# A gated MLP on one core: the DMA transposes of x take 256 columns in place of 128

## The chip, the core and the metric

The kernel runs on one core of a Trainium2 chip. The core has five engines that run side by side: TensorE (matrix products, PE in the profile; its weight loads are the row PEld), VectorE (DVE), ScalarE (ACT), GpSimd (POOL) and SyncE (SP), which in this kernel issues every DMA. Sixteen DMA engines move the data between the chip's main memory (HBM) and the on-chip memory. The metric is the device time of one execution in microseconds (us); lower is better.

## The reference

For x of 2048 rows by 1024 columns and three weight matrices, all bf16:

```
g = x @ w_gate          # 2048 x 3584
u = x @ w_up            # 2048 x 3584
h = gelu(g) * u         # gelu in its tanh form
out = h @ w_down        # 2048 x 1024
```

## The kernel before, in words

Both stages use Strassen's scheme, in which a product of 2x2 blocks needs seven block products and a number of sums of blocks (the tiles s1 to s4 are sums of weight blocks, t1 to t4 sums of blocks of x). The sums are made by VectorE and GpSimd, copies out of TensorE's accumulators (the eight banks) mostly by ScalarE.

The 2048 rows of x are taken as two passes p of 1024, and each pass as two halves c of 512 rows. TensorE contracts over the partition dimension, so x is needed transposed: for each (p, c) eight blocks, one for each 128 of the 1024 columns, each a tile of 128 partitions by 512 rows of x. They are kept in `XT[p, c][ko]`, ko from 0 to 7 (lines 72, 73 and 87 to 94):

- (0, 0) lies in xT0. It is turned by TensorE itself at the start (`turn`, L798), from four plain loads `xn`.
- (0, 1) lies in four slots `x` of two blocks each.
- (1, 0) lies in xT1, and (1, 1) in the first eight of the fourteen rows of the tile h01, which is used for other things later.

The last three are filled by DMA transposes, 24 in all, each 512 rows by 128 columns, issued on SyncE's queue by `transposing` (L806). The order of that queue is the order of the program. At its head stand the four loads of xn, the loads of the weights for the first block of columns (L814, in three parts) and the second one (L145). Then come the eight transposes of (0, 1), the loads of the third block of weights (L143), and the sixteen transposes of pass 1. The list `turns` (L833) gives the order of these sixteen: first blocks 0 to 3 of (1, 1) and (1, 0) in turn, then blocks 4 to 7 of (1, 1), then blocks 4 to 7 of (1, 0). `turn_some(n)` issues the next n of the list: four at once (L840), the others between steps of the first two units of work, by the table `AHEAD` (L48), where (n, part) is the unit and the place within it. Between these groups the queue holds the stores of finished blocks of h to HBM (L227, in `times`), each of which waits for VectorE to have written its block.

Who reads the transposed blocks around these steps:

- `plain` (L842) multiplies blocks by the first weights, two blocks of x after each other for each of four accumulators.
- `sums_t` (L153) makes t1 to t4 of pass 0 on VectorE, a block at a time, and casts blocks 4 to 7 of (0, 1) on ScalarE (tb).
- `two_sums` (L938) makes t1 to t4 of pass 1 on GpSimd, two blocks in an instruction.
- `product` (L229) with `raw_first` and `raw_second` (L233, L238) takes four blocks in order for each of two accumulators: blocks 0 to 3 of xT1, then 4 to 7. In the second unit (n is 1 in `ahead_of_p4`, L1087) the first such products of pass 1 run: 16 on blocks 0 to 3, then eight on blocks 4 to 7, four for each accumulator.

After these first units the kernel goes on with joint units for both passes up to some 385 us, and then with the second product, out = h @ w_down.

Of the kernel before, what the change touches and what calls it, by code (L numbers as in the profile page):

```python
# [10 lines left out]
def kernel(  # L11
# [13 lines left out]
    P = nc.NUM_PARTITIONS  # L25
# [7 lines left out]
    x2 = x.flatten_outer_dims()  # L33
# [4 lines left out]
    NKB = Dm // P  # L38
    KH = NKB // 2
    NFB = Df // P  # L40
    NJ = NFB // 2
    N = 512
    NS = N // P
    NPASS = S // (2 * N)
    NU = NFB // 2
    NWARM = 7
    JOINT = 3
    AHEAD = {(0, -2): 4, (0, -1): 2, (0, 0): 2, (0, 1): 2, (1, -2): 2}  # L48
    DIVIDED7 = 5
    STAY = range(11, 14)  # L50
    KEEPS = [(u, n) for u in range(5, NU) for n in range({7: 2, 9: 2, 11: 2, 13: 3}.get(u, 1))]
# [19 lines left out]

    xT = [xpool.tile([P, NKB, N], bf16, name=f"xT{p}") for p in range(NPASS)]
    XT = {(p, 0): [xT[p][:, k] for k in range(NKB)] for p in range(NPASS)}
    h = [[None, None], [None, None]]

    wdn = w_down.rearrange("(kh j p) d -> p kh j d", kh=2, p=P)

    def slot(shape, dtype, name):
        return kpool.tile(shape, dtype, name=name, tag="k")
# [7 lines left out]
    def late_half(p):  # L87
        if p:
            tile = hpool.tile([P, NJ, N], bf16, name="h01")
            XT[p, 1] = [tile[:, k] for k in range(NKB)]  # L90
            x_late.append(tile[:, :NKB])
        else:
            tiles = [slot([P, 2, N], bf16, "x") for _ in range(KH)]
            XT[p, 1] = [tiles[k // 2][:, k % 2] for k in range(NKB)]

    def new_h(kh, c):
        h[kh][c] = hpool.tile([P, NJ, N], bf16, name=f"h{kh}{c}")
# [20 lines left out]
    def snap(ps, name):  # L118
        t = slot([P, N], f32, name)
        nc.scalar.copy(out=t, in_=ps)  # L120
        return t
# [10 lines left out]
    def load_w(u, slots=False):  # L132
        f0 = u * 2 * P
        if slots:
            w = [[slot([P, KH, 2 * P], bf16, "w") for _ in range(2)] for _ in range(2)]
        else:
            tile = wpool.tile([P, 2, NKB, 2 * P], bf16, name="w")
            w = parts(tile)
        for i, src in enumerate((w_gate, w_up)):
            src = src[:, f0 : f0 + 2 * P].rearrange("(ko ki) f -> ki ko f", ki=P)  # L140
            if slots:
                for half in range(2):
                    nc.sync.dma_start(out=w[i][half], in_=src[:, half * KH : (half + 1) * KH])  # L143
            else:
                nc.sync.dma_start(out=tile[:, i], in_=src)  # L145
        return w
# [6 lines left out]
    def sums_t(p, eng, place):  # L153
        K = range(KH)
        lo, hi = [[XT[p, c][k0 : k0 + KH] for c in range(2)] for k0 in (0, KH)]

# [72 lines left out]
    def product(ps, lhs, rhs, start):  # L229
        for k in range(KH):  # L230
            matmul(ps, lhs[:, k, :], rhs[k], start and k == 0, k == KH - 1)

    def raw_first(e, p, w):  # L233
        for i in range(2):
            product(e[i], w[i][0][:, :, :P], XT[p, 0][:KH], True)
        return [snap(e[i], "p1") for i in range(2)]

    def raw_second(c, p, w):  # L238
        for i in range(2):
            product(c[i], w[i][1][:, :, :P], XT[p, 0][KH:], True)  # L240

# [110 lines left out]
    def joint_ops(u, E, F):  # L352
# [28 lines left out]
        def raw(name, p, i):  # L381
            ops["P1" + name] = lambda: product(E[p][i], w[i][0][:, :, :P], XT[p, 0][:KH], True)

# [419 lines left out]
            ks = slice(ks.start, ks.stop)  # L803
            (on_act if i == 1 else on_dve)(out=xT[0][:, ks, i * P : (i + 1) * P], in_=tp[:, ks])

    def transposing(p, c, ko):  # L806
        r0 = (2 * p + c) * N
        nc.sync.dma_start_transpose(  # L808
            out=XT[p, c][ko], in_=x2[r0 : r0 + N, ko * P : (ko + 1) * P]
        )  # L810

    def load_wf(queue, k0, k1):
# [12 lines left out]
    for k0, k1 in ((0, 2), (2, 5), (5, NKB)):  # L825
        load_wf(nc.sync, k0, k1)
    w = load_w(1)
    late_half(0)
    for ko in range(NKB):
        transposing(0, 1, ko)  # L830
    ahead = load_w(2, True)
    late_half(1)
    turns = [(c, ko) for ko in range(KH) for c in (1, 0)] + [(c, ko) for c in (1, 0) for ko in range(KH, NKB)]  # L833

    def turn_some(n):
        for c, ko in turns[:n]:
            transposing(1, c, ko)
        del turns[:n]

    turn_some(4)  # L840

    def plain(ps, c, kos, parts=1):  # L842
        n = N // parts
# [221 lines left out]
    with tc.manual_schedule(engines={ENG.Activation}):  # L1065
        for n, (u, p) in enumerate(items):
# [4 lines left out]
            def aside(part):  # L1071
# [4 lines left out]
                for v in loads.get((n, part), ()):  # L1076
                    ws[v] = load_w(v, True)
                turn_some(AHEAD.get((n, part), 0))
                if (n, part) == (1, -2):
# [125 lines left out]
```

## Time and profile before

| what | value |
|---|---|
| runs shown (three) | 530.77, 529.16, 531.03 us, median 530.77 |
| profiled execution | 528.45 us |
| its span, first to last instruction | 526.7 us |
| granted TensorE clock | 1.000 |
| TensorE busy | 520.9 us (99%) |
| GpSimd, VectorE, ScalarE busy | 337.5, 390.6, 293.9 us |
| DMA transposes: x, h01, xT1 | 8 each, first issue 8.4 us, last 47.4 us |
| one of them on SyncE's queue, median | 1.25 to 1.26 us |
| from issue to landing, shortest, median, longest | 2.5, 2.9, 5.9 us |

The profile is of one execution. In the rows a line like L124 is the line of the kernel's source; a line such as L124, L103 or L106 is a helper that records most of TensorE's, VectorE's or GpSimd's operations, so groups are told apart by their tiles (`bank<-xT,w` reads xT and w and writes an accumulator). "SPq" is SyncE's queue: the time of an issue is how long the instruction held the queue, and the landing of the data comes after it. An arrow in brackets, as in `[1.03 <-DMA xT<-in_x_dram]`, gives the idle time ahead of the row and what ended it. The chain of work that ended last is followed back from the last instruction, at each step to what released it. In the tables of windows the columns are the window, its length, then the busy time and number of instructions of TensorE, its weight loads, VectorE, ScalarE and GpSimd, the granted clock, the mean busy share of the DMA engines and GB/s.

### The profile page before, as it was taken

The page shows a single profiled execution, that of the slowest core. Times are in us where ns is not written, and L with a number is a line of the kernel's source. Part 1 is how long each engine was busy: PE and PEld are TensorE (multiplying, and loading weights), DVE is VectorE, ACT ScalarE, POOL GpSimd, SP SyncE. Part 2 cuts the span into 40 slices and gives each one's busy share as a digit, 9 for nine tenths or more (in the row PEclk, how much of TensorE's full clock was granted, in tenths as well). Part 3 has the DMA queues.
Part 4 walks back from the last instruction along what each step waited for, and adds up shares of the span by engine and source line. Part 5 has one row for each costly group of instructions (what it writes and reads, how often), then busy time and mean ns, then how long its engine had stood idle before and what let it go on. Part 6 is the DMA issues. An engine that isn't in the chain of part 4 may idle for free.

```text
span 526.7 us, 7917 instructions
## 1 busy us (share of the span) xinstructions
PE 520.9 (99%) x2389; PEld 367.9 (70%) x2389; DVE 390.6 (74%) x598; ACT 293.9 (56%) x542; POOL 337.5 (64%) x339
## 2 busy tenths in 40 slices
PE   8999999999999999999999999999999999999997
PEld 4575777767677676767676676754688885488887
DVE  2984553587888889897988899896879226966934
ACT  2545655767687686878787786851135601142430
POOL 1169899999999999999999999940000000000694
PEclk9999999999999999999999999999999999999999
DMA  9755233042625266363727354999986999983732
GB/s 245 161 133 131 73 110 110 21 120 76 205 70 191 83 218 209 120 217 113 257 96 229 136 184 145 338 371 415 386 273 200 392 402 371 394 307 101 237 132 71
DMA packets 103114, 105.91 MB, mean 201 GB/s; under 512 B 19744, under 2 KB 81184, under 8 KB 103072
## 3 DMA queue, kind: packets, MB, share of 16 engines
q1 hardware_dynamic: 103072, 105.41, 61.1%
q8 instruction: 19, 0.31, 0.3%
q14 instruction: 23, 0.19, 0.1%
HBM read 72.61 MB, written 29.62 MB: 194 GB/s over the span
## 4 chain that ended last, share of the span: by engine, by line
PE 91%; SPq 3%; DVE 2%; DMA 2%; issue 1%; ACT 0%; DVEq 0%
PE bank L124 91%; SPq L808 2%; DMA xT<-in_x_dram 1%; DVE t L103 1%; DMA w<-in_w_up_dram 1%; DVE s L103 1%; SPq L227 0%; DVE h L103 0%; SPq L794 0%; ACT g L218 0%; DVE sum L103 0%; SPq L814 0%; DVE st L103 0%; DVE bank L103 0%; DVEq L103 0%
## 5 line engine op out<-in xcount | busy, mean ns | idle before, releaser
L124 PE MATMUL bank<-h,s 128*128 128x512 f32 x500 | 132.6, 395 | 0.0
L106 POOL TENSOR_TENSOR q<-q 128x256 fp32r<-128x256 f32 x28 | 27.0, 997 | 144.2 <-DMA q<-td 143.7
L124 PE MATMUL bank<-xT,w 128*128 128x512 bf16 (+1 forms) x472 | 109.0, 377 | 1.1 <-DMA xT<-in_x_dram 1.0
L124 PEld LDWEIGHTS bank<-h,s 128*128 128x128 f32 x500 | 93.9, 188 | 21.1
L124 PEld LDWEIGHTS <-w 128*128 128x128 bf16 x504 | 45.2, 98 | 60.6 <-issue 13.7
L106 POOL TENSOR_TENSOR s<-w 128x512 fp32r<-128x512 bf16 (+1 forms) x76 | 77.8, 1039 | 11.0 <-DMA w<-in_w_gate_dram 11.0
L124 PE MATMUL bank<-t,s 128*128 128x512 f32 x276 | 76.5, 400 | 0.0
L124 PE MATMUL bank<-q 128*128 128x512 f32 x264 | 65.6, 390 | 0.0
L124 PEld LDWEIGHTS bank<-t,s 128*128 128x128 f32 x276 | 51.9, 188 | 12.2
L120 ACT COPY p<-bank 128x512 f32<-128x512 f32 x72 | 40.7, 589 | 30.7 <-PE bank L124 26.8
L124 PEld LDWEIGHTS bank<-q 128*128 128x128 f32 x264 | 49.6, 188 | 10.4
L103 DVE TENSOR_TENSOR q<-h,h 128x512 fp32r<-128x512 bf16 x56 | 38.2, 682 | 16.5 <-DMA h<-hd 16.5
L120 ACT COPY u<-bank 128x512 f32<-128x512 f32 x62 | 35.8, 589 | 18.8 <-PE bank L124 18.6
L106 POOL TENSOR_TENSOR s<-s,s 128x256 fp32r<-128x256 f32 x60 | 44.8, 770 | 1.6
L103 DVE TENSOR_TENSOR xz<-bank,xz 128x512 f32<-128x512 f32 x44 | 30.2, 691 | 18.5 <-PE bank L124 14.3
L124 PEld LDWEIGHTS <-h 128*128 128x128 bf16 x224 | 21.8, 98 | 26.5 <-issue 0.5
L106 POOL TENSOR_TENSOR s<-w,s 128x512 fp32r<-128x512 bf16 (+1 forms) x37 | 39.4, 1082 | 0.0
L106 POOL TENSOR_TENSOR s<-s,w 128x512 fp32r<-128x512 f32 (+1 forms) x37 | 37.3, 1023 | 0.9
L115 ACT CAST tb<-raw 128x512 fp32r<-128x512 bf16 x28 | 16.9, 632 | 36.6 <-DMA raw<-in_w_down_dram 24.9
L106 POOL TENSOR_TENSOR m<-raw,m 128x512 fp32r<-128x512 bf16 x28 | 34.5, 1233 | 2.2
L103 DVE TENSOR_TENSOR bank<-bank,u 128x512 f32<-128x512 f32 x49 | 33.7, 688 | 0.0
L103 DVE TENSOR_TENSOR v<-bank,v 128x512 f32<-128x512 f32 x44 | 29.2, 684 | 2.1 <-PE bank L124 1.7
(122 smaller groups left out, 912.5 us busy)
## 6 DMA issues: line engine op xcount, KB each, us to landing
raw<-in_w_down_dram SPq DMA_DIRECT2D x68, 256.0 KB, 3.9
q<-td SPq DMA_DIRECT2D x66, 256.0 KB, 5.4
td<-m SPq DMA_DIRECT2D x42, 256.0 KB, 2.8
hd<-o SPq DMA_DIRECT2D x80, 128.0 KB, 1.7
h<-hd SPq DMA_DIRECT2D x17, 512.0 KB, 7.0
hd<-h SPq DMA_DIRECT2D x30, 128.0 KB, 1.8
h<-hd SPq DMA_DIRECT2D x5, 768.0 KB, 8.3
out_dram<-st SPq DMA_DIRECT2D x30, 128.0 KB, 4.4
```

The lines of the kernel that those rows point to most:

```text
L103: nc.vector.tensor_tensor(out=out, in0=a, in1=b, op=op)
L106: nc.gpsimd.tensor_tensor(out=out, in0=a, in1=b, op=op)
L115: nc.scalar.copy(out=t, in_=src)
L120: nc.scalar.copy(out=t, in_=ps)
L124: nc.tensor.matmul(ps, lhsT=lhs, rhs=rhs, start=start, stop=stop, skip_group_check=True)
L808: nc.sync.dma_start_transpose(out=XT[p, c][ko], in_=x2[r0 : r0 + N, ko * P : (ko + 1) * P])
```

## The change

Each transposing transfer takes 256 columns of x: two neighbouring blocks, ko and ko + 1, in one transfer, written to two neighbouring rows of the same tile. So there are 12 transfers in place of 24. The destination of a pair comes from the new table `XT2`. The order is kept, two blocks at a time, and so is the place of each group among the loads and stores on SyncE's queue: the counts of `AHEAD` and of the first `turn_some` are halved, and the two groups of two that stood next to each other in the queue, (0, -1) and (0, 0), are now the one at (0, -1). Nothing else is changed; on the other engines the instructions and their order are the same. (Three lines are added, so most line numbers of the changed kernel are higher by three.)

```diff
-    AHEAD = {(0, -2): 4, (0, -1): 2, (0, 0): 2, (0, 1): 2, (1, -2): 2}
+    AHEAD = {(0, -2): 2, (0, -1): 2, (0, 1): 1, (1, -2): 1}
...
+    XT2 = {(p, 0): lambda k, p=p: xT[p][:, k : k + 2] for p in range(NPASS)}
...
             x_late.append(tile[:, :NKB])
+            XT2[p, 1] = lambda k: tile[:, k : k + 2]
         else:
             tiles = [slot([P, 2, N], bf16, "x") for _ in range(KH)]
             XT[p, 1] = [tiles[k // 2][:, k % 2] for k in range(NKB)]
+            XT2[p, 1] = lambda k: tiles[k // 2]
...
-    def transposing(p, c, ko):
+    def transposing(p, c, k0):
         r0 = (2 * p + c) * N
         nc.sync.dma_start_transpose(
-            out=XT[p, c][ko], in_=x2[r0 : r0 + N, ko * P : (ko + 1) * P]
+            out=XT2[p, c](k0), in_=x2[r0 : r0 + N, k0 * P : (k0 + 2) * P]
         )
...
-    for ko in range(NKB):
+    for ko in range(0, NKB, 2):
         transposing(0, 1, ko)
     ahead = load_w(2, True)
     late_half(1)
-    turns = [(c, ko) for ko in range(KH) for c in (1, 0)] + [(c, ko) for c in (1, 0) for ko in range(KH, NKB)]
+    turns = [(c, ko) for ko in range(0, KH, 2) for c in (1, 0)] + [(c, ko) for c in (1, 0) for ko in range(KH, NKB, 2)]
...
-    turn_some(4)
+    turn_some(2)
```

## The prediction

> **What bounds the kernel now.** I read the summary of busy shares first, then TensorE's own list of waits, then the chain of work that ended last, then SyncE's queue in order of time, and last the windows that show how full the DMA engines are while x is transposed.
>
> TensorE is the bound, and its list of waits has three entries:
>
> ```profile
> PE 520.9 (99%) x2389; PEld 367.9 (70%) x2389; DVE 390.6 (74%) x598; ACT 293.9 (56%) x542; POOL 337.5 (64%) x339
> ...
> PE bank L124 <- DMA xT<-in_x_dram: 1.0, 1, 1.0
> PE bank L868 <- PEq L1189: 0.8, 1, 0.8
> PE bank L801 <- DMA xn<-in_x_dram: 0.7, 1, 0.7
> ```
>
> Two belong to the start and are not touched. The third is the only one that a transposing transfer causes: 1.03 us, in the order of time of TensorE:
>
> ```profile
> 44.68 4.39 PE L124 MATMUL bank<-xT,w 128*128 128x512 bf16 x19
> 50.11 1.24 PE L124 MATMUL bank<-xT,w 128*128 128x512 bf16 x5 [1.03 <-DMA xT<-in_x_dram]
> ```
>
> Nineteen of the 24 raw products run, and the twentieth needs block 7 of xT1. TensorE stands from 49.08 to 50.11. The chain that ended last says who was late: from 28.9 us to 50.1 us it is nothing but SyncE's queue, then TensorE without a break:
>
> ```profile
> 45.83 0.30 SPq L227
> 46.18 1.12 SPq L808
> 47.36 2.71 DMA xT<-in_x_dram
> 50.11 473.53 PE bank L124 x2153
> ```
>
> The reader is to see that one transfer, issued at 47.36, lands 2.71 us later, and that from there TensorE has work to 523.6. SyncE's queue itself, from 20.8 us:
>
> ```profile
> 20.81 1.13 SPq L143 DMA_DIRECT2D w<-in_w_gate_dram  x2
> ...
> 29.34 1.12 SPq L808 DMA_TRANSPOSE h<-in_x_dram  x1
> 30.51 1.25 SPq L808 DMA_TRANSPOSE xT<-in_x_dram  x1
> 31.81 1.26 SPq L808 DMA_TRANSPOSE h<-in_x_dram  x1
> 33.11 1.26 SPq L808 DMA_TRANSPOSE xT<-in_x_dram  x1
> 34.47 1.00 SPq L227 DMA_DIRECT2D hd<-h  x2
> 35.52 5.04 SPq L808 DMA_TRANSPOSE h<-in_x_dram  x4
> 40.66 1.00 SPq L227 DMA_DIRECT2D hd<-h  x2
> 41.71 2.43 SPq L808 DMA_TRANSPOSE xT<-in_x_dram  x2
> 44.25 1.89 SPq L227 DMA_DIRECT2D hd<-h  x3
> 46.18 2.43 SPq L808 DMA_TRANSPOSE xT<-in_x_dram  x2
> ```
>
> A transfer of 128 columns holds the queue 1.12 to 1.27 us, two of them start to start 2.47 to 2.63, 2.53 in the mean. Windows of those stretches (the last two numbers are the DMA engines' share and GB/s):
>
> ```profile
> 17.00:20.80 3.80, 3.80 (x19) 1.75 (x18) 3.80 (x7) 2.24 (x4) 0.00 (x0) 1.00 0.44 77
> 29.30:34.40 5.10, 5.10 (x25) 3.21 (x24) 4.95 (x10) 1.37 (x3) 3.76 (x5) 1.00 0.50 129
> 35.50:40.60 5.10, 5.10 (x24) 4.19 (x23) 2.58 (x4) 3.02 (x6) 5.10 (x5) 1.00 0.51 130
> ```
>
> The DMA engines are half idle: the pace is set by the issuing queue. One transfer uses at most 0.51 x 5.10 / 4 = 0.65 us of them.
>
> **The change part by part.**
>
> *The price C of a transfer of 256 columns on SyncE's queue.* The trace has none. Lower end 1.25 us, as one of 128 columns (all of the time is per instruction); nothing excludes less, but 2 x 0.65 = 1.3 us of DMA work would then set the pace. Upper end 2.53, two single ones (all of it per row or block); a longer one is not excluded and is the rival that loses. The nearest rows are the plain loads of w: two with four blocks of 128x256 take 1.13 us to issue, 0.57 each, and one with eight blocks takes 0.74 at 6.04 us: 1.3 times, where the row count doubles. That gives 1.25 x 1.3 = 1.6. I take 1.8, because the 0.65 us of data of a transposing transfer is a larger part of its 1.25 us than that of a load's issue, and keep 1.3 and 2.53 for the range.
>
> [...]
>
> *SyncE's queue.* Twelve issues instead of 24; all else on it keeps its order (loads of w, then pairs and stores of h in turn). Of the twelve, four turn the second half of the first 1024 rows (8.44 to 20.8 us). They sit behind the loads of w, the first of the eight singles takes 2.59 us for it, so I count no saving from them, only that they land no later. The other eight save 2.53 - C each: 8 x 0.73 = 5.8 us at C = 1.8. The last pair's issue would end at 48.61 - 5.8 = 42.8. It can't go earlier than the stores ahead of it allow: the third of the three at 44.25 reads an h that VectorE makes from 38.41 to 39.69, so the last pair starts after about 40.1 at the earliest; both floors are far below 49.
>
> *Landing.* A single lands 2.71 us after its issue began, 1.46 after its end; the pair's second half adds 0.65, so 2.1. The last pair lands at 42.8 + 2.1 = 44.9, against 48.86, when TensorE comes to block 6 (blocks 6 and 7 are now one landing, one product of 0.22 us earlier than the wait of before). **The 1.03 us go.** This holds while 48.61 - 8 (2.53 - C) + 2.1 is below 48.86, that is for C up to 2.3.
>
> *Coarser landings.* A consumer of the first block of a pair now waits for both. For the raw products of the second half (32 from 17.91, 0.221 us each) block pair 6, 7 is needed at 17.91 + 24 x 0.221 = 23.2. ScalarE's casts show the landings of before by their waits (block 7 at 22.33). Even at C = 2.53 a pair lands at 22.3 + 0.65 = 23.0, before that. VectorE reads the same pair for t2 at 22.1 and could slip 0.6 us or so; its t2 is next used by TensorE at 24.63, its t4 at 35.40. GpSimd's sums read pairs of blocks in one instruction already (128x1024). So I cost this at nothing; without that cover it would be 0.65 us.
>
> *Work that is released earlier.* The loads of w for the third block of columns (1 MB, at 20.81) go out no later; GpSimd reads them at 30.8. The stores of h go out earlier and remove waits of VectorE (2.0 us) and ScalarE (2.0 us) on them around 36 us, which TensorE doesn't feel.
>
> *What follows the wait.* TensorE's next steps must move up by the whole 1.03 us. GpSimd's t4 starts at 54.14 after 1.62 us of idle time, once ScalarE's casts of the same room end at 54.01; those follow a gelu that follows TensorE's late product. They move up together, and GpSimd is free from 52.52, so 1.03 of the 1.62 can be had. t1, t2 and t3 are ready at 52.52, TensorE uses t3 some 3.7 us after 54.60 and t4 at 62.07. From 48.71 on SyncE waits for VectorE's h as before. No new wait comes in place of the old one.
>
> *Sum.* The profiled execution took 528.45 us (span 526.7 and 1.75 around it): 528.45 - 1.03 = 527.42. The median of the runs is 530.77, which is 2.32 above the profiled one; with that, **529.74 us**, 0.2% less.
>
> **The rivals.**
> [...]
> [...]
> 3. *More than the 1.03 us.* The shown runs are 0.7 to 2.6 us longer than the profiled one, and nothing says where. If that lies in this same wait, it goes too: 530.77 - 1.03 - 2.3 = 527.4. Against it: any part of the run can hold it, above all the DMA-heavy second half (up to 415 GB/s).
>
> **How the numbers follow.** About 0.5% (2.65 us) is what a measurement of this kernel can tell from no change; the shown runs alone spread 1.9 us. Forecast 0.68, with 529.16 - 1.03 = 528.1 to 531.03 - 1.03 = 530.0 as its own range; rival 1 0.15, up to 531.6; rival 2 0.09; rival 3 0.08. The range leaves out rival 2 and the far end of rival 3: 528.0 to 531.7. Faster by over 0.5%: rival 3 and a little scatter, 0.08. Slower by over 0.5%: rival 2 and the scatter on rival 1, 0.11. Within: 0.81.
>
> **What would show it.** Right: twelve transposing issues of 1.3 to 2.3 us on SyncE's queue, the last one ending before 44 us; TensorE's list without an entry on xT; its stretch that began at 50.11 joined to the one from 44.68; GpSimd's idle time before t4 near 0.6 us in place of 1.62; the chain no longer through SyncE from 28.9 to 50 us. Wrong: issues over 2.3 us, a wait of TensorE on xT (or on x at 17.9 to 23.2), or a new wait after 50 us, on t4 or in the second half, that takes the 1.03 us back.

## The result and the profile after

The changed kernel takes 526.91 us in the median of nine executions (526.36 to 527.40), the kernel before 529.08 in nine beside it (528.32 to 531.03). The ratio is 0.9955, with a 95% interval of 0.9940 to 0.9969: 2.2 us faster. That is just inside the 0.5% that the prediction called no change, but the interval excludes no change, and 526.91 lies below the prediction's range (528.0 to 531.7). The profiled execution took 526.39 us, with a span of 524.6.

TensorE's list of waits, of the changed kernel, has lost its entry on xT:

```profile
PE bank L871 <- PEq L1192: 0.8, 1, 0.8
PE bank L804 <- DMA xn<-in_x_dram: 0.3, 1, 0.3
```

In order of time, the 24 raw products of that place are one stretch (23 were recorded), and the next one follows at 49.01 us in place of 51.00. First the row of the kernel before, then two of the changed kernel:

```profile
51.00 2.20 PE L124 MATMUL bank<-t,sa 128*128 128x512 f32 x8
...
44.00 5.35 PE L127 MATMUL bank<-xT,w 128*128 128x512 bf16 x23
49.01 2.19 PE L127 MATMUL bank<-t,sa 128*128 128x512 f32 x8
```

SyncE's queue in order of time: the twelve transfers, the last issue over at 39.3 us and not at 48.6 (most stores of h are left out).

```profile
7.97 7.67 SPq L811 DMA_TRANSPOSE x<-in_x_dram  x4
15.69 2.60 SPq L146 DMA_DIRECT2D w<-in_w_gate_dram  x2
18.34 1.05 SPq L146 DMA_DIRECT2D w<-in_w_up_dram  x2
19.43 1.84 SPq L811 DMA_TRANSPOSE h<-in_x_dram  x1
21.32 2.10 SPq L811 DMA_TRANSPOSE xT<-in_x_dram  x1
...
24.58 1.24 SPq L811 DMA_TRANSPOSE h<-in_x_dram  x1
25.87 1.29 SPq L811 DMA_TRANSPOSE xT<-in_x_dram  x1
...
28.30 2.63 SPq L811 DMA_TRANSPOSE h<-in_x_dram  x2
...
32.71 1.24 SPq L811 DMA_TRANSPOSE xT<-in_x_dram  x1
34.38 3.67 SPq L230 DMA_DIRECT2D hd<-h  x3
38.10 1.24 SPq L811 DMA_TRANSPOSE xT<-in_x_dram  x1
```

Away from the loads a pair holds the queue 1.24 to 1.3 us, about as long as one block did (1.12 to 1.27): from one block to two the price did not grow. Behind the loads of w it is more: the first two pairs of x took 3.34 and 1.60, the two at 19.43 and 21.32 took 1.84 and 2.10.

The chain that ended last no longer goes through this queue. Its first line, by engine:

```profile
PE 98%; DMA 1%; issue 0%; SPq 0%; DVE 0%
```

The spans differ by 2.1 us, and the rows say where: at the first product on xT0 the changed kernel is 0.61 us ahead (6.66 against 7.27, the two rows below), by the landing of the plain loads xn (TensorE waits 0.27 us for them, against 0.74), which the change doesn't touch; at the next step after the 24 raw products it is 1.99 ahead, and it stays so (its last step begins at 521.64, against 523.66). So 1.38 us came in between, most of it at the wait of 1.03 us: from the first of the 24 products to the step after them before took 6.32 us, after 5.01. Whether the 0.61 belongs to the change is the first question for the experiments.

```profile
7.27 10.80 PE L124 MATMUL bank<-xT,w 128*128 128x256 bf16 x56
...
6.66 10.76 PE L127 MATMUL bank<-xT,w 128*128 128x256 bf16 x55
```

### The profile page after: what moved, and what is told of

It is laid out like the page before. It is cut to its first block, busy times and chain, and to the rows that moved or that the text cites. A ratio compares the mean times of both kernels' runs of the same rounds, so it can differ in the third digit from the quotient of the medians.

```text
span 524.6 us, 7866 instructions
## 1 busy us (share of the span) xinstructions
PE 518.7 (99%) x2356; PEld 368.0 (70%) x2389; DVE 390.6 (74%) x598; ACT 293.6 (56%) x542; POOL 336.9 (64%) x339
## 4 chain that ended last, share of the span: by engine, by line
PE 98%; DMA 1%; issue 0%; SPq 0%; DVE 0%
PE bank L127 98%; DMA xn<-in_x_dram 1%; SPq L797 0%; PE bank L804 0%; DVE st L106 0%
## 5 line engine op out<-in xcount | busy, mean ns | idle before, releaser
L127 PE MATMUL bank<-xT,w 128*128 128x512 bf16 (+1 forms) x446 | 106.8, 376 | 1.5
```

The source lines that it names most:

```text
L127: nc.tensor.matmul(ps, lhsT=lhs, rhs=rhs, start=start, stop=stop, skip_group_check=True)
```

## The experiments

Theory A: the gain is the late landing of the last block of xT1 and what it causes, and nothing else. It has two rivals. B: the gain goes by the number of transfers saved. C: part of it is the earlier start, as an effect of the change. D is a later addition to A, from the second profile of the kernel before (a granted clock of 0.50 after the waits): long waits also halve TensorE's clock in some executions. Ratios are to the kernel before, run beside each experiment on the same chip.

**The kernel before once more.** No edit.

> The kernel before, unchanged, for a second profile of it. Theory A (all of the gain is the landing of the last block of xT1; what the run's first 7 us add is scatter between executions): ratio 1.000 within 0.002; TensorE again stands on xT for 0.5 to 2 us near 49 to 50 us, and the first product on xT0 starts anywhere between 6.6 and 7.3 us (7.27 in the first profile, 6.66 in that of the changed kernel), with a longer wait on xT where it starts earlier. Theory C (a part of the gain of some 0.6 us is the earlier start of the changed kernel): it starts at 7.2 to 7.3 again.

Ratio 0.9994 (0.9979 to 1.0009). TensorE in order of time, second profile of the kernel before:

```profile
7.01 10.68 PE L124 MATMUL bank<-xT,w 128*128 128x256 bf16 x55
...
39.22 3.96 PE L124 MATMUL bank<-t,s 128*128 128x512 f32 x16 [0.20 <-ACT g L218]
...
44.83 4.06 PE L124 MATMUL bank<-xT,w 128*128 128x512 bf16 x17
50.24 0.38 PE L124 MATMUL bank<-xT,w 128*128 128x512 bf16 x1 [1.35 <-DMA xT<-in_x_dram]
51.41 1.84 PE L124 MATMUL bank<-xT,w 128*128 128x512 bf16 x5 [0.79 <-DMA xT<-in_x_dram]
52.69 3.42 PE L124 MATMUL bank<-t,sa 128*128 128x512 f32 x8
```

The start is at 7.01, and not again at 7.27 as C had it: it scatters (6.66 to 7.66 over the twelve profiles here). The wait is 2.14 us in two pieces, as two blocks landed late, and the eight products after it took 3.42 us in place of 2.19. SyncE's queue shows why the blocks were late: the pair of issues that had taken 2.43 us at 41.71 now took 1.5 us more.

```profile
42.01 3.92 SPq L808 DMA_TRANSPOSE xT<-in_x_dram  x2
```

The windows of this execution give the reason for the slow products (the clock is the third number from the end):

```profile
51.00:52.00 1.00, 0.59 (x3) 0.29 (x3) 0.12 (x1) 0.00 (x0) 1.00 (x1) 0.95 0.81 251
52.00:53.00 1.00, 1.00 (x5) 0.49 (x2) 0.57 (x1) 0.40 (x1) 0.04 (x1) 0.50 0.04 11
53.00:54.00 1.00, 1.00 (x4) 0.76 (x3) 0.64 (x1) 1.00 (x3) 0.00 (x0) 0.50 0.00 0
54.00:55.00 1.00, 1.00 (x4) 0.81 (x3) 0.75 (x2) 1.00 (x3) 0.00 (x0) 0.50 0.00 0
55.00:56.00 1.00, 1.00 (x5) 0.58 (x5) 0.00 (x0) 0.30 (x1) 0.57 (x1) 0.84 0.28 96
```

After the two waits, 1.35 and 0.79 us with a product between them, the granted clock is half (0.50) for about 3.4 us (0.05 + 3 x 0.5 + 0.16 = 1.7 us lost). This execution took 531.36 us.

**Singles, but the last two ahead of three stores.**

```diff
-    AHEAD = {(0, -2): 4, (0, -1): 2, (0, 0): 2, (0, 1): 2, (1, -2): 2}
+    AHEAD = {(0, -2): 4, (0, -1): 2, (0, 0): 2, (0, 1): 4}
```

> Still 24 transfers of 128 columns; only the last two (blocks 6 and 7 of xT1) go out ahead of three stores of h and not behind them. Theory A: the last issue ends near 46.7 in place of 48.6 us and lands near 48.2, before TensorE comes to block 7 at 49.08, so the wait on xT goes and the whole gain comes: 1.3 to 2.2 us less than before (ratio 0.9958 to 0.9975). Theory B (fewer and larger transfers are what gains, by the queue's or the DMA engines' time): no gain, ratio 1.000 within 0.001.

Ratio 0.9962 (0.9949 to 0.9975): most of the gain with 24 transfers, so B falls as the whole story. A had said that the wait on xT goes, but the profiled execution still waited: 0.92 us on xT, because the four issues took 6.47 us and not 5.0, and 0.49 us near 39 us on a gelu:

```profile
36.84 0.59 ACT L120 COPY p<-bank 128x512 f32<-128x512 f32 x1 [2.69 <-DMA hd<-h]
38.12 0.63 ACT L218 ACTIVATE g<-sum 128x512 f32<-128x512 f32 x1 [0.69 <-DVE sum L103]
```

ScalarE's copy waits 2.69 us for a store of h, whose room it reuses; that store stood in SyncE's queue behind the transposes. So the late stores reach TensorE too.

**Only the last four as two pairs.** On the changed kernel, with a width for each transfer; the other 20 are single again (only the core of the edit is shown):

```diff
-    turns = [(c, ko) for ko in range(0, KH, 2) for c in (1, 0)] + [(c, ko) for c in (1, 0) for ko in range(KH, NKB, 2)]
+    turns = [(c, ko) for ko in range(KH) for c in (1, 0)] + [(1, ko) for ko in range(KH, NKB)] + [(0, 4), (0, 6)]
+    pair = lambda c, ko: c == 0 and ko >= KH
```

> Only the last four transfers (blocks 4 to 7 of xT1) are made two of 256 columns; the other 20 stay single, so 22 in place of 24. Theory A: the last issue ends near 46.2, lands near 48.0, before 48.86: the whole gain, 1.3 to 2.2 us less than before (ratio 0.9958 to 0.9975). Theory B: two of the twelve issues saved, a sixth of the measured 2.17 us, 0.4 us (ratio 0.999).

Ratio 0.9966 (0.9954 to 0.9979), far from the 0.999 of B. The profile has 0.32 us of waiting left. That would explain why the ratio is a little short of the changed kernel's, but the two intervals overlap.

**All pairs, the last one two stores later.** `turn_some(1)` moves from (1, -2) to the head of the branch n == 1 in `ahead_of_p4`:

```diff
-    AHEAD = {(0, -2): 2, (0, -1): 2, (0, 1): 1, (1, -2): 1}
+    AHEAD = {(0, -2): 2, (0, -1): 2, (0, 1): 1}
...
                 elif n == 1:
+                    turn_some(1)
```

> All twelve pairs as in the changed kernel, but the last one (blocks 6 and 7 of xT1) goes out two stores later, behind the store of the h that VectorE writes near 45.3 us. Theory A: its issue begins near 46.5 to 47, it lands near 49.6 to 50.3, TensorE wants it near 48.0 and waits 1.6 to 2.3 us, which costs up to 0.3 more than the wait shows: the gain is gone, ratio to before 0.999 to 1.001. Theory B: twelve transfers still, so the gain stays, ratio 0.9955 to 0.997.

Ratio 0.9973 (0.9959 to 0.9987): about half of the gain is gone. A had said all of it (0.999 to 1.001), B none (0.9955 to 0.997), so the number alone decides for neither. The wait came as A foresaw (1.6 to 2.3 us):

```profile
50.63 1.46 PE L127 MATMUL bank<-xT,w 128*128 128x512 bf16 x6 [1.66 <-DMA xT<-in_x_dram]
```

With 1.66 us of waiting in its profile, this kernel is still faster than the kernel before. If A holds, its error is the size set against that wait: the wait of before must then be more than 1.03 us in most executions. The second profile (2.14 us) fits that; no run shows the wait of the others.

**The changed kernel once more; only x in pairs; pass 1 in fours.** The second makes only the first eight transfers four pairs and leaves the rest single, in the order of before. The third takes 512 columns for pass 1 (only the list is shown, against the changed kernel):

```diff
-    turns = [(c, ko) for ko in range(0, KH, 2) for c in (1, 0)] + [(c, ko) for c in (1, 0) for ko in range(KH, NKB, 2)]
+    turns = [(1, 0), (0, 0), (1, KH), (0, KH)]
```

> The changed kernel, unchanged, for a second profile and on one chip with the next three. Theory A (the gain is the wait on the last block of xT1, with what it brings along): ratio 0.9955 within 0.0015; no wait of TensorE on xT; the first product on xT0 starts anywhere between 6.6 and 7.7 us and the time follows that start. Theory D (a long wait on xT also halves the granted clock in some executions of the kernel before, as in its second profile): here no execution lies more than 1.5 us over the fastest.

> Only the first eight transfers (the second half of the first rows, tiles x) become four of 256 columns; all 16 of pass 1 stay single. Theory A: SyncE's queue is 4 to 5 us ahead from 16 us on, the last block of xT1 lands near 45 us, the wait is gone: ratio 0.9945 to 0.997, as with all twelve pairs. Theory B (the gain goes by the number of transfers saved): four of the twelve, a third of it, ratio 0.9985.

> The x tiles in pairs as in the changed kernel, pass 1 in four transfers of 512 columns, so 8 in place of 12. Theory A: nothing waits for the queue any more, so the time is that of the changed kernel, ratio to before 0.994 to 0.997; an issue takes between 1.25 us (a price per instruction) and 2.6 us (the data of four blocks at 0.65 us). Theory B: fewer is faster again, ratio 0.992 to 0.994.

The ratios are 0.9955 (0.9940 to 0.9969), 0.9951 (0.9934 to 0.9968) and 0.9954 (0.9937 to 0.9971). Four pairs far ahead of the place that waits bring the whole gain, and 8 transfers bring no more than 12: B is refuted, and no variant beats the changed kernel beyond the intervals. A transfer of 512 columns held the queue 1.31 to 2.07 us, and 4.19 behind the loads. In none of the three profiles does TensorE wait on xT; with x in pairs the 24 products are one stretch again:

```profile
44.55 5.35 PE L127 MATMUL bank<-xT,w 128*128 128x512 bf16 x24
```

The changed kernel's second profile starts at 7.28, as the first one of before did (7.27), and took 527.11 us against 528.45. So the start is not earlier by the change, and C falls too; with equal starts these two profiles differ by 1.34 us.

**Filling the wait, and making it longer.** The first puts five products on constants ahead of the product on block 7, in the kernel before. The second, on the kernel before, issues the last two transfers later (the first two edits below). The third does the same and also fills both waits, five products ahead of block 6 and five ahead of block 7 (the whole diff):

```diff
-    AHEAD = {(0, -2): 4, (0, -1): 2, (0, 0): 2, (0, 1): 2, (1, -2): 2}
+    AHEAD = {(0, -2): 4, (0, -1): 2, (0, 0): 2, (0, 1): 2}
...
                 elif n == 1:
+                    turn_some(2)
                     p1 = [raw_first(e, 1, loaded(v)) for e, v in ((Eb, 2), (D, 1))]
-                    raw_second(K, 1, loaded(2))
+                    for k in range(KH):
+                        for _ in range({2: 5, 3: 5}.get(k, 0)):
+                            nc.tensor.matmul(K[1], lhsT=warm[:, :P], rhs=warm, start=True, stop=True)
+                        matmul(K[0], loaded(2)[0][1][:, k, :P], XT[1, 0][KH + k], k == 0, k == KH - 1)
+                    product(K[1], loaded(2)[1][1][:, :, :P], XT[1, 0][KH:], True)
                     finish_raw(2, 1, K, p1[0])
```

> The kernel before with five products of 128x512 on constants, written to the accumulator whose own products start afterwards, put ahead of the product on block 7 of xT1, where TensorE waits: 1.1 us of work that adds nothing to the output. Theory D: the wait is filled, no gap is long enough to halve the clock, and the executions over 530.4 us (11 of the 35 last shown of before) are gone; the median falls by 0.2 to 0.6 us (ratio 0.9989 to 0.9996). Theory A without D: the slow third comes from elsewhere and stays, the median is the same or up to 0.3 us higher.

> The kernel before with the last two single transfers (blocks 6 and 7 of xT1) issued one step later, behind two more stores of h, so that TensorE waits on both blocks, for some 2 to 3 us in all, nearly always. Theory A: the time without any wait, 519.8 us after the first product on xT0, plus the waits and 0.3 us for each: 1 us over the undisturbed executions of before, 530.2 to 530.8 us. Theory D (waits of that length halve the granted clock for some 3.4 us, which costs 1.7): more than half of the executions have a mean clock of 0.997 or less and lie near 532, the median 531.5 to 532.5.

> As single_late, with five products of 128x512 on constants ahead of the products on block 6 and five more ahead of block 7 (2.2 us of work that adds nothing to the output), so that TensorE has something to do until the blocks land. Theory D: no execution with a mean clock of 0.997 or less; the blocks land as late, so the median is 530.0 to 531.2 us, at least 0.5 below single_late. Theory A without D: no difference in the clock between the two, and fill_late is the same or slower by up to 1 us, as its extra work is only partly hidden.

The first gave a ratio of 1.0000 (0.9988 to 1.0013), where D had foreseen 0.9989 to 0.9996. It settles little: in its profile the wait came at block 6, ahead of the fill, and on that chip only one of 20 executions of before had a low clock. The other two tell more:

| kernel | median, us | ratio to before (95%) | executions with a mean clock of 0.997 or less |
|---|---|---|---|
| last two issued later | 531.14 | 1.0032 (1.0012 to 1.0051) | 7 of 11 |
| the same, waits filled | 530.43 | 1.0018 (1.0005 to 1.0030) | 0 of 11 |

The filled one does 2.2 us more work, and none of its executions shows the low clock. Its median is 0.7 us lower, as D has it, though the intervals overlap, and in its one profile the blocks also landed earlier (block 6 was multiplied 43.1 us after the first product on xT0, against 44.0). So the counts carry the argument, not the medians; the median of the kernel with the longer waits lies between what A (530.8 at most) and D (531.5 at least) had said. The kernel before had a mean clock of 0.997 or less in 15 of the 88 executions run with these experiments, each of 530.75 us or more; the three kernels without the wait (changed, x in pairs, fours) in none of 30. Most of these 30 ran on the chip where the kernel before shows it only once in 20. On the chip where it shows it in 10 of 47, the three kernels with a shorter wait or one wait alone (last two early, last four as pairs, last pair late) show it in none of 36.

**One sum for all.** For each profiled execution, its time less the start of the first product on xT0, in us (the two filled kernels follow below the table):

| kernel | start | time less start | over 519.8 | waits of TensorE on xT and gelu |
|---|---|---|---|---|
| changed, two profiles | 6.66, 7.28 | 519.73, 519.83 | 0 | none |
| x in pairs; fours | 7.19; 7.38 | 519.82; 519.77 | 0 | none |
| last four as pairs | 7.66 | 520.37 | 0.6 | 0.32 |
| before, first profile | 7.27 | 521.18 | 1.4 | 1.03 |
| last pair late | 7.55 | 521.61 | 1.8 | 1.66 |
| singles, last two early | 6.73 | 521.70 | 1.9 | 0.92 + 0.49 |
| last two singles late | 7.33 | 523.60 | 3.8 | 1.89 + 0.88 + 0.40 |
| before, second profile | 7.01 | 524.35 | 4.6 | 1.35 + 0.79 + 0.20, half clock 1.7 |

Every time is the start, plus 519.8, plus the waits, plus 0.15 to 0.35 for each wait, plus the clock. The two filled kernels are each 2.9 over; their waits are 1.07 + 0.21 and 0.65, and the products on constants take 1.1 and 2.2. Nothing above 0.35 us for each wait is left over for the transfers themselves.

## Why the prediction was wrong

The place, the wait and the queue behind it were right; two terms of the sum had the wrong size. The saving, "The 1.03 us go", was too small: 2.2 us went in the median. And the base, 530.77, was too high: nine executions gave 529.08. The points in turn:

- *The bound and the place.* Right: TensorE without a break from the wait on, SyncE's queue as what is late, and no new wait after 50 us.
- *The price of a pair.* Taken at 1.8 us, measured 1.24 to 1.3 away from the loads: the lower end of the bounds. The queue saves more for it, but the sum doesn't depend on it once the pair lands in time. The row that the estimate was scaled from, 0.74 us for a load of eight blocks, was one of two: the other load of that size, at 6.83, took 1.57. The step from 1.6 to 1.8, by the share of the data in an issue's time, was the author's estimate; no run shows that share for a load. The upper bound, 2.53, is not borne out for this transfer: 128 KB, 256 KB and the shortest of 512 KB held the queue 1.25, 1.24 and 1.31 us.
- *"I count no saving" from the four pairs of x.* Wrong: the eight singles held the queue 12.3 us, the four pairs 7.7, and with x alone in pairs that brings the whole gain.
- *Landing.* Foreseen 3.9 us from the start of the issue (1.8 and 2.1), measured 3.1 to 4.1 on xT1. The last pair's issue was foreseen to begin after about 40.1 at the earliest and began at 38.10, since the h ahead of it was ready earlier as well.
- *Coarser landings at nothing.* Right: ScalarE waits once for x, 1.1 us, in place of 2.5 us in four waits. GpSimd's idle time ahead of t4 fell from 1.62 to 0.33 us, near the 0.6 foreseen.
- *The term that was mis-sized:* "The 1.03 us go." The row gives the gap between modelled ends of products; the stretch around it shows 1.31, and 1.34 remain between two executions with equal starts. And 1.03 was one execution's wait. The second profile has 2.14, because one pair of issues near 42 us took 3.92 us and not 2.43. Five of the six profiles with single transfers at that place, all but the first, show such a delay (3.5 to 3.9, or 6.47 for four in place of 5.0), and so do the last two singles of x in pairs (3.23). So the first profile looks like the short case; how the 2.2 us of the median divide was not measured. What causes the delay stays open. In two of these profiles, the second of before and the last two early, the DMA view (`--dma`) shows a transfer of 0.02 MB of a queue called "instruction" between 41 and 51 us; the first profile has one there too, without the delay.
- *"which TensorE doesn't feel".* Wrong in part: the late stores held TensorE up by 0.2 to 0.5 us in four profiles of single transfers, through ScalarE and a gelu.
- *The base.* The median of 530.77 was of three executions; nine, 35, 20 and 21 gave 529.08, 529.70, 529.23 and 529.39. Of the miss (529.74 against 526.91) 1.7 us are the base and 1.1 the gain. The 2.32 us between the profiled execution and that median were taken along as a constant. They are not one: the second profile of before took 2.9 us more than the first, by its longer wait and its halved clock. That the same holds for the other executions above the profile is inferred from the sum, not shown.
- *The rivals.* The third had named this ("If that lies in this same wait, it goes too", 527.4, chance 0.08). It was the better forecast and got too small a chance, though its 527.4 also rests on the base that was too high, so its nearness to 526.91 is in part luck. Against it stood only that any part of the run could hold the difference; that the chain ran through a queue with no slack for 21 us should have weighed more. The first two, a pair at the price of two singles and a dearer one, are refuted by the price of a pair, 1.24 to 1.3 us away from the loads. No run shows, away from the loads, the 2.53 us or more for a pair on which their part of the range, up to 531.6, and their chances rest.

## What to carry to other kernels

When one queue has been busy without a break up to the wait that it causes, as SyncE's was here for 21 us, the wait in one profile is a sample and not a price: it was 1.03 us in the first profile of before, and 2.14 in the second, where two issues ahead of it took 3.92 us in place of 2.43. Removing it here also removed scatter (all executions of the changed kernel lie within 1.5 us, those of before within 4.7), and a mean clock of 0.997 or less, which before had in 15 of 88 executions, came in none of 18 of the changed kernel. What counted was when the last transfer landed that TensorE waited for; an earlier saving on the same queue served as well as one at the place itself (0.9951 with x alone in pairs, 0.9966 with the last four as pairs). And a base of three executions should not be carried to a tenth of a microsecond.

## What the runs showed that was not expected

- A transposing transfer's issue time did not grow from one block of 128 columns to two (1.25 and 1.24 us). With four it was 1.31 at best and 2.02 at worst where no load is ahead.
- Waits of TensorE that add up to 2.1 us were followed by half of the granted clock for about 3.4 us in one profile. A mean clock that fits this (0.997 or less) shows in part of the executions, 7 of 11 with the waits made longer and 15 of 88 in the kernel before, and in none of 11 with the waits filled by products on constants.
- The first product on xT0 started between 6.66 and 7.66 us with the same instructions ahead of it, after waits of TensorE of 0 to 1.21 us on the plain loads: 1 us of scatter that a comparison of two single profiles can't tell from a gain.
